# Two edits to a fused attention and mixture-of-experts kernel: a longer planned distance in the merge of routing and products, and a split last copy

## The chip, the cores and the metric

One NeuronCore of a Trainium2 chip runs the whole program. The time is the device time of one execution in microseconds (us). Five engines work side by side, each through its own instructions in program order: TensorE (PE in the profile), VectorE (DVE), ScalarE (ACT), GpSimd (POOL) and SyncE (SP, which here only starts loads). An instruction that waits holds back everything behind it on its engine.

## The reference, cut to what matters

```python
scores = np.where(mask, q @ k.T / 8, -1e9)     # 8 batches, 8 heads, 576 positions, window 64
x = (softmax(scores) @ v).reshape(4608, 512)
logits = x @ w_gate                            # 8 experts
for idx in np.argsort(-logits.flatten()):      # best (token, expert) pair first
    tok, e = idx // 8, idx % 8
    if assigned[tok] < 0 and counts[e] < 576:  # every expert takes 576 tokens
        assigned[tok] = e; counts[e] += 1
for e in range(8):
    out[assigned == e] = np.maximum(x[assigned == e] @ w1[e], 0) @ w2[e]   # 512 -> 1024 -> 512
```

## The kernel before

The first 165 us or so are the attention, which the change does not touch. After it, eight experts are closed one after the other. For the expert that fills up next, a **search** finds the threshold of its 576th token: four rounds, in each of which DVE compares all maxima with 15 thresholds (`G`, line 593), PE counts them in nine small matmuls (the tally, line 629), and DVE turns the counts into the next thresholds (lines 635 to 770). A **listing** then makes the 576 token numbers: PE sums positions (lines 931, 932), DVE and ACT build one-hot tables, PE multiplies them (18 matmuls, line 1020; 8 of line 1032), and DVE writes the list `idx` (line 1038). With the list, POOL gathers the tokens (`xg`, line 1202, five transfers). PE transposes them (`tp`, line 1240, four matmuls a tile) into one of two PSUM buffers (`bufs=2`), ACT copies the rounded high half out (`xh`, line 1190), and DVE subtracts it from the same `tp` to leave the low half (`xh`, line 1194). Tiles 0 and 1 are transposed as a pair, then 2 and 3, then 4.

An expert's **products** are the h layer (line 1302, in units: a 256-column unit has four 512-wide matmuls and four 256-wide ones) and the o layer: 16 matmuls of line 1336 and 96 of line 1346, all 512 wide. The first unit needs both halves of tiles 0 and 1. Weights come in 1024-column chunks: SP loads `st`, ACT copies the high half `wh` (line 1129) and starts the low half `wl` (line 1143), and an adding DMA that POOL starts completes `wl` (line 1145).

While PE works on the o layer of one expert, the listing of the next one ends and the search for the one after that begins; so rounds 1 to 4 of a search lie at the end of an o layer and in the h layer behind it.

The order of all this is made by a planner that runs when the program is built. `Streams` is a heap of generators; each yields the time that it believes its step takes, and whichever is due first issues its next instructions. `busy(dt, engine)` keeps one account for each engine and returns when the work would end. Due times are only an ordering device: on the chip each engine follows the order and waits where data are late. The planned costs that matter below, in ns: a 512-wide product 228, a pair of transposes 355 each, a tally 350, the matmuls of line 1020 630, those of line 1032 255, a copy of a weight chunk on ACT 1050, a copy of `xh` 520 on ACT and 600 on DVE; on the DMA account a gather or a put 700, a load 1350, an adding DMA 2650, with 2000 more until data land. POOL is charged 1300 for a gather, 1040 for a put, 650 for an adding DMA.

`SLACK[p]` is what the planner adds between a DVE step and the PE step that reads it, and between a PE step and the DVE step that reads it: twice in each tally (lines 624 and 633), in the listing of p at lines 929, 934, 1016, 1025, 1028 and 1036, and for p = 6 once more (line 969). The search that runs during expert p's products belongs to p + 1 and takes `SLACK[p + 1]`; the listing of p takes `SLACK[p]`. Of the places:

```python
yield max(slack, copied - self.clock() if not r else 0)   # tally, before the nine matmuls
yield self.busy(350) + 200 + slack                        # tally, before DVE reads the counts
yield self.dve(340) + slack                               # listing, before lines 931 and 932
yield self.busy(255) + 200 + slack                        # listing, before DVE writes idx
```

A tile pair is due by the gathers (`there`); then it waits until a routing matmul has been issued (`joins > n0`) or a latest time `t0` has come. The second copy of a pair is due 700 ns after the first:

```python
dt = self.busy(355)
self.spawn(evac(a, 128 if a < 4 else 64, t), dt + 150 + 700 * n)
```

Of the kernel before, what the change touches and what calls it, by code (L numbers as in the profile page):

```python
# [15 lines left out]
AF = mybir.ActivationFunctionType  # L16
# [7 lines left out]
E = 8  # L24
# [416 lines left out]
ALONE = [mybir.EngineType.DVE]  # L441
NG = 4
WIDE = 1.25
SLACK = (0, 0) + (100,) * 6
U32 = mybir.dt.uint32


class Routing:
# [297 lines left out]
    def guessed(self, p, code, one4, copied):  # L746

        nc, tile_ = self.nc, self.wk.tile
        tab, slack = self.gtab, SLACK[p]
        if p == 1:  # L750
# [124 lines left out]
    def steps(self, p):  # L875

        nc, wk, V = self.nc, self.wk, self.V
        m, best, one = self.m, self.best, self.one
        slack = SLACK[p]
        tile_ = wk.tile  # L880
# [179 lines left out]
JOIN = ((800, -1800), (2000, 900), (3300, 2000))  # L1060
SECOND = 27500
FIRST = 6500


class Experts:
# [29 lines left out]
    def load(self, p, ei):  # L1095
# [7 lines left out]
        def fetch(i):  # L1103
# [8 lines left out]
            if p == 0 and i == 3:  # L1112

                t = max(t, self.clock() + self.busy(0, "pool") + FIRST)
            there[i] = t
# [133 lines left out]
    def steps(self, p, idx):  # L1249
        nc, fw = self.nc, self.fw  # L1250
# [61 lines left out]
        def put(a, o):  # L1312
            ot = fw.tile([128, DM], FT, name="ot", bufs=3)
            m = 128 if a < 4 else 64
            if a < 4:
                nc.scalar.activation(ot, o, AF.Copy)  # L1316
                self.busy(500, "act")
            else:
                t = fw.tile([64, DM], FT, name="low")
                nc.scalar.activation(t, o[64:128], AF.Copy)  # L1320
                yield self.busy(500, "act") + 150
                self.busy(600, "dve")
                nc.vector.tensor_tensor(ot[0:64], o[0:64], t, OP.add)
            yield max(600, self.sent - self.clock())
            nc.gpsimd.indirect_dma_start(out=self.out[5 * p + a],  # L1325
                                         out_offset=IndirectOffsetOnAxis(ap=idx[0:m, a:a + 1], axis=0),
                                         in_=ot[0:m], in_offset=None)
            self.busy(TOKENS, "dma")
            self.sent = self.clock() + self.busy(1040, "pool")


        o = self.ps.tile([128, DM], FT, name="o", bufs=2)
        for f in range(NF):
            yield lambda: (p, NCH + f // 2) in self.W
            for n, w in enumerate(self.W[p, NCH + f // 2]):
                nc.tensor.matmul(o, hh[:, f, 512:], w[:, 512 * (f % 2):512 * (f % 2) + 512],  # L1336
                                 start=(f == 0 and n == 0), stop=(f == NF - 1 and n == 1))
                yield self.busy(228)
        self.spawn(put(4, o), 100)
        for a in range(4):  # L1340
            o = self.ps.tile([128, DM], FT, name="o", bufs=2)
            k = 0
            for f in range(NF):
                wh, wl = self.W[p, NCH + f // 2]
                for wt, ht in ((wh, hh), (wl, hh), (wh, hl)):
                    nc.tensor.matmul(o, ht[:, f, 128 * a:128 * a + 128], wt[:, 512 * (f % 2):512 * (f % 2) + 512],  # L1346
                                     start=(k == 0), stop=(k == 23))
                    k += 1
                    yield self.busy(228)
            self.spawn(put(a, o), 100)  # L1350
# [99 lines left out]
```

## Time and profile before

| | us |
|---|---|
| median of 3 runs | 622.74 (622.03 to 623.49) |
| the profiled execution | 619.33 |
| its span, first to last instruction | 617.4 |
| PE busy in the span | 591.4 (96%) |
| DVE, ACT, POOL busy | 397.6, 372.8, 186.2 |

The trace is of one execution, and all times of rows count from its first instruction. Matmuls overlap in it, so a busy PE is not a PE at its peak: a gap shows in the distance between the starts of successive matmuls.

### The profile page before, as it was taken

Reading aid. Unit: us, or ns where it says so; the run is one execution under the profiler, and the core shown is the slowest. Engines: PE = TensorE matmul, PEld = TensorE weight load, DVE = VectorE, ACT = ScalarE, POOL = GpSimd, SP = SyncE. Lnnn points to the kernel's source line nnn. Section 1 sums busy time; section 2 is a strip of 40 time slices with the busy share of each in tenths; the row PEclk is TensorE's granted clock in tenths of the full one; section 3 lists DMA queues with packets and bytes.
Section 4 is the critical chain, followed back from the end, with each engine's and each line's share of the span. In section 5 each row is a group of like instructions: output and inputs, shape, how many; then the busy total and the mean of one; then the engine's idle time right before and its main releaser. Section 6 shows DMA issues by size and latency. Waiting matters only on the chain.

```text
span 617.4 us, 15509 instructions
## 1 busy us (share of the span) xinstructions
PE 591.4 (96%) x5750; PEld 505.6 (82%) x5750; DVE 397.6 (64%) x1832; ACT 372.8 (60%) x798; POOL 186.2 (30%) x245
## 2 busy tenths in 40 slices
PE   8999899996599999999999999999999999999996
PEld 6777778785499789878987997898889789889984
DVE  6888888987786487468646846773695467705400
ACT  6998889996465387267537734762685275614410
POOL 1433445341341262044116203610630173011011
PEclk9999999998599999999999999999999999999998
DMA  8999999961598699189748937992896689410001
GB/s 315 358 363 365 362 390 376 355 223 71 158 254 179 216 209 251 34 299 224 171 143 239 247 75 255 210 235 68 270 240 124 200 214 316 184 44 34 2 27 51
DMA packets 44950, 128.85 MB, mean 209 GB/s; under 512 B 4672, under 2 KB 5312, under 8 KB 44864
## 3 DMA queue, kind: packets, MB, share of 16 engines
q1 hardware_dynamic: 30592, 79.00, 35.7%
q0 software_dynamic: 13984, 48.25, 33.8%
q8 instruction: 46, 0.75, 0.5%
q10 hardware_dynamic: 288, 0.52, 0.3%
q14 instruction: 40, 0.33, 0.2%
HBM read 82.14 MB, written 18.87 MB: 164 GB/s over the span
## 4 chain that ended last, share of the span: by engine, by line
PE 49%; issue 17%; DVE 4%; POOL 4%; DMA 1%; ACT 1%; POOLq 0%; DVEq 0%
PE h L1302 25%; PE o L1346 18%; PE o L1336 4%; POOL out L1325 2%; PE rps L629 1%; DVE xh L1194 1%; PE tp L1240 1%; POOL xg L1202 1%; POOL wl L1145 1%; DMA xg<-xs,idx 1%; PE rps L1020 1%; ACT xh L1190 0%; DMA xs<-x 0%; DVE G L593 0%; POOL rest L1202 0%
## 5 line engine op out<-in xcount | busy, mean ns | idle before, releaser
L1302 PE MATMUL h<-xh,wh 128*128 128x320 f32 (+2 forms) x800 | 160.9, 333 | 0.2 <-DVE xh L1194 0.2
L1302 PEld LDWEIGHTS h<-xh,wh 128*128 128x128 f32 x800 | 124.1, 188 | 5.1 <-DVE xh L1194 0.4
L1346 PE MATMUL o<-wh,hl 128*128 128x512 f32 x256 | 101.4, 396 | 0.0
L1346 PE MATMUL o<-wl,hh 128*128 128x512 f32 x256 | 100.5, 392 | 0.0
L1346 PE MATMUL o<-wh,hh 128*128 128x512 f32 x256 | 100.3, 392 | 0.0
L1325 POOL DMA_INDIRECT out<-ot,idx x40 | 40.1, 1003 | 198.5 <-DVE q L906 82.6
L141 ACT ACTIVATE pe<-st,mx 128x128 f32<-128x128 f32 x288 | 92.0, 393 | 5.2 <-DVE mx L136 4.9
L1302 PE MATMUL h<-xh,wl 128*128 128x256 f32 (+1 forms) x512 | 89.7, 296 | 0.0
L1302 PEld LDWEIGHTS h<-xh,wl 128*128 128x128 f32 x512 | 78.7, 188 | 4.4
L1145 POOL DMA_DIRECT2D wl<-st x51 | 46.0, 1024 | 83.6 <-ACT wl L1143 28.7
L1316 ACT ACTIVATE ot<-o 128x512 f32<-128x512 f32 x32 | 19.2, 598 | 83.2 <-PE o L1346 78.3
L1129 ACT ACTIVATE wh<-st 128x1024 fp32r<-128x1024 f32 x64 | 67.3, 1051 | 3.4 <-DMA st<-w 3.4
L136 DVE CUSTOM_DVE_ANT_0 st<-Sp,mask 128x128 f32<-128x128 f32 x288 | 63.8, 285 | 7.3 <-PE Sp L128 6.2
L1346 PEld LDWEIGHTS o<-wl,hh 128*128 128x128 f32 x256 | 48.1, 188 | 9.7
L1346 PEld LDWEIGHTS o<-wh,hh 128*128 128x128 f32 x256 | 48.1, 188 | 9.4
L1346 PEld LDWEIGHTS o<-wh,hl 128*128 128x128 f32 x256 | 48.1, 188 | 9.3
L1143 ACT ACTIVATE wl<-wh 128x1024 fp32r<-128x1024 f32 x51 | 54.0, 1058 | 1.1
L1266 ACT ACTIVATE hh<-h 128x320 fp32r<-128x320 f32 (+1 forms) x72 | 30.8, 428 | 30.9 <-PE h L1302 30.4
L1263 DVE TENSOR_TENSOR sum<-h,sum 128x256 f32<-128x256 f32 x56 | 23.6, 421 | 40.0 <-ACT sum L1261 38.6
L150 ACT ACTIVATE pt<-Tp 128x512 f32<-128x512 f32 x72 | 42.2, 587 | 8.3 <-PE Tp L148 8.3
L1202 POOL DMA_INDIRECT xg<-xs,idx x32 | 32.3, 1010 | 46.4 <-DVE eq L944 38.8
L1271 DVE SCALAR_TENSOR_TENSOR hl<-h,hh 128x256 fp32r<-128x256 f32 x72 | 30.3, 421 | 23.7 <-ACT hh L1266 23.5
(215 smaller groups left out, 1022.3 us busy)
## 6 DMA issues: line engine op xcount, KB each, us to landing
st<-w SPq DMA_DIRECT2D x59, 512.0 KB, 6.4
wl<-st POOLq DMA_DIRECT2D x51, 512.0 KB
xs<-x SPq DMA_DIRECT2D x36, 256.0 KB, 5.4
VO<-v SPq DMA_DIRECT2D x6, 1168.0 KB, 18.1
Q<-q SPq DMA_DIRECT2D x6, 1152.0 KB, 13.4
K<-k SPq DMA_DIRECT2D x6, 1152.0 KB, 16.3
VT<-vt SPq DMA_DIRECT2D x6, 1152.0 KB, 17.3
st<-w POOLq DMA_DIRECT2D x5, 512.0 KB
```

What stands on the lines that cost most here:

```text
L136: nc.vector.tensor_tensor_reduce(st[:, h, :], Sp[h % 2][:, h // 2], mk, scale=-0.125, scalar=3.0e38, op0=OP.add, op1=OP.min, accum_out=mx[ ...
L141: nc.scalar.activation(pe[:, h, :], st[:, h, :], AF.Exp, bias=mx[:, h:h + 1], scale=-1.0)
L150: return pt, lambda: nc.scalar.activation(pt.rearrange("p h q -> p (h q)"), Tp, AF.Copy)
L1129: nc.scalar.activation(hi, st[i], AF.Copy)
L1143: nc.scalar.activation(lo, hi.bitcast(FT), AF.Copy, scale=-1.0)
L1145: nc.gpsimd.dma_start(lo.bitcast(FT), st[i], accum_op=OP.add)
L1202: nc.gpsimd.indirect_dma_start(out=g[a][0:n], out_offset=None, in_=self.xs, in_offset=IndirectOffsetOnAxis(ap=idx[0:n, a:a + 1], axis=0))
L1266: nc.scalar.activation(hh[:, f, c0:c1], h, AF.Relu)
L1271: nc.vector.scalar_tensor_tensor(t, h[:, a - c0:b - c0], 0.0, hh[:, f, a:b].bitcast(FT), op0=OP.max, op1=OP.subtract)
L1302: nc.tensor.matmul(h[:, 0:w], wv[:, cc, 128 * (f % 2):128 * (f % 2) + 128], x[:, cc, x0:x0 + w], start=(k == 0), stop=(k == 4 * len(terms) ...
L1325: nc.gpsimd.indirect_dma_start(out=self.out[5 * p + a], out_offset=IndirectOffsetOnAxis(ap=idx[0:m, a:a + 1], axis=0), in_=ot[0:m], in_off ...
L1346: nc.tensor.matmul(o, ht[:, f, 128 * a:128 * a + 128], wt[:, 512 * (f % 2):512 * (f % 2) + 512], start=(k == 0), stop=(k == 23))
```

## The change

`SLACK` goes from 100 to 400 ns for p = 2 to 6 (third to seventh search and listing); p = 0, 1 and 7 keep their values. The last tile of the last expert (a = 3) is copied from PSUM in two halves of 256 columns, one by ACT and one by DVE, instead of whole by ACT.

```diff
-SLACK = (0, 0) + (100,) * 6
+SLACK = (0, 0) + (400,) * 5 + (100,)
...
+HALF = 256
...
             ot = fw.tile([128, DM], FT, name="ot", bufs=3)
             m = 128 if a < 4 else 64
-            if a < 4:
+            if p == E - 1 and a == 3:
+                nc.scalar.activation(ot[:, 0:HALF], o[:, 0:HALF], AF.Copy)
+                nc.vector.tensor_copy(ot[:, HALF:], o[:, HALF:])
+            elif a < 4:
                 nc.scalar.activation(ot, o, AF.Copy)
                 self.busy(500, "act")
```

## Rows read from the trace of the kernel before

**Rows 1.** The page: busy time, share of the span, instructions of PE.
```profile
PE 591.4 (96%) x5750; PEld 505.6 (82%) x5750; DVE 397.6 (64%) x1832; ACT 372.8 (60%) x798; POOL 186.2 (30%) x245
```

**Rows 2.** Timeline of PE, 264 to 300 us: start, length, instructions, idle before and releaser.
```profile
278.49 0.79 PE L1240 MATMUL tp<-identr,xg 128*128 128x128 f32 x8
...
282.27 0.79 PE L1240 MATMUL tp<-identr,xg 128*128 128x128 f32 x8
282.90 0.70 PE L1302 MATMUL h<-xh,wh 128*128 128x512 f32 x2
283.94 0.59 PE L629 MATMUL rps<-G,one 128*128 128x60 bf16 x9 [0.34 <-DVE G L593]
284.36 0.71 PE L1302 MATMUL h<-xh,wh 128*128 128x512 f32 x2
284.91 0.64 PE L1302 MATMUL h<-xh,wl 128*128 128x256 f32 x4
...
289.59 0.43 PE L629 MATMUL rps<-G,one 128*128 128x60 bf16 x9
289.85 0.39 PE L1302 MATMUL h<-xh,wh 128*128 128x320 f32 x1
```

**Rows 3.** Timeline of PE, 449 to 453 us: the same place three experts later.
```profile
451.24 0.59 PE L629 MATMUL rps<-G,one 128*128 128x60 bf16 x9 [0.31 <-DVE G L593]
```

**Rows 4.** The chain that ended last, 254 to 285 us: products between routing steps.
```profile
258.41 5.89 PE o L1346 x26
...
264.38 4.19 PE o L1346 x18
...
269.11 0.77 PE o L1346 x3
...
270.03 8.62 PE o L1346 x37
```

**Rows 5.** Timeline of ACT, 252 to 300 us: two copies of tokens, then weights.
```profile
279.16 1.09 ACT L1190 ACTIVATE xh<-tp 128x512 fp32r<-128x512 f32 x2 [1.37 <-PE tp L1240]
280.13 1.06 ACT L1129 ACTIVATE wh<-st 128x1024 fp32r<-128x1024 f32 x1
```

**Rows 6.** Timeline of DVE, 240 to 300 us: from first to second round.
```profile
279.79 0.69 DVE L1194 TENSOR_TENSOR xh<-tp,xh 128x512 fp32r<-128x512 f32 x1 [3.06 <-ACT xh L1190]
...
280.89 0.69 DVE L1194 TENSOR_TENSOR xh<-tp,xh 128x512 fp32r<-128x512 f32 x1
...
282.70 0.21 DVE L692 STREAM_TRANSPOSE num<-ps 128x32 f32<-128x32 f32 x1
282.94 0.16 DVE L768 TENSOR_REDUCE d<-num 128x1 f32<-128x8 f32 x1
...
283.41 0.79 DVE L593 TENSOR_TENSOR G<-m,thr 128x300 bf16<-128x300 f32 x2
```

**Rows 7.** Timeline of ACT, 533 to 538 us: weights between two copies of tokens.
```profile
533.95 1.05 ACT L1129 ACTIVATE wh<-st 128x1024 fp32r<-128x1024 f32 x1
534.90 0.59 ACT L1190 ACTIVATE xh<-tp 128x512 fp32r<-128x512 f32 x1
```

**Rows 8.** Timeline of PE, 536 to 538 us: a transpose that waits.
```profile
536.91 0.53 PE L1240 MATMUL tp<-identr,xg 128*128 128x128 f32 x4 [0.25 <-DVE xh L1194]
```

**Rows 9.** Timeline of POOL, 252 to 312 us: the first three adding DMAs.
```profile
277.85 2.85 POOL L1145 DMA_DIRECT2D wl<-st  x3
```

**Rows 10.** Timeline of PE, 501 to 508 us: the seventh expert.
```profile
501.41 0.79 PE L1240 MATMUL tp<-identr,xg 128*128 128x128 f32 x8
...
507.01 1.07 PE L1302 MATMUL h<-xh,wh 128*128 128x512 f32 x4
```

**Rows 11.** Timeline, 611 us to the end: the last copy.
```profile
611.34 0.60 ACT L1316 ACTIVATE ot<-o 128x512 f32<-128x512 f32 x1 [4.89 <-PE o L1346]
```

**Rows 12.** Groups by line: copies of half the width.
```profile
L1261 ACT ACTIVATE sum<-h 128x256 f32<-128x256 f32 x56 | 21.4, 382 | 29.5 <-PE h L1302 29.5
L1263 DVE TENSOR_TENSOR sum<-h,sum 128x256 f32<-128x256 f32 x56 | 23.6, 421 | 40.0 <-ACT sum L1261 38.6 <-issue 1.0
```

## The prediction

> **What bounds the kernel now.** I read the page first, then the waits of PE, then PE's timeline around each place where PE waits, then ACT and DVE at the same times. On the page the reader is to see that PE is busy for 96% of the span [rows 1]: only PE's gaps can give time back, and anything that makes PE wait costs in full. In the o and h layers the gap worth seeing is before the second round's tally. The h layer opens at 282.90 with two products; at 0.227 us each the tally could begin at 283.36 and be over 0.26 later, as the third round's is (289.59 to 289.85). It begins at 283.94, waits in its middle for the second half of `G`, and the next product starts at 284.36 instead of 283.62 [rows 2]. I take 0.7 us (0.65 to 0.74) for this stall. The same place three experts later shows the same releaser [rows 3]; there are four of them, in the o layers of the second to fifth expert. All four together are 2.8 us, and that is the most that a longer distance can recover. The third round shows no wait, and neither does any other tally from the third search on.
>
> **The change: what is moved.** I work out the order from the planner's rules, counting due times from S, the start of an o layer, in us. They say only what stands before what. Before: lines 931 and 932 are due at 9.41, line 1020 at 13.81, line 1032 at 15.07, the list at 15.70, the first pair of transposes and the first tally at 23.61. With a product each 0.228 that puts 16 + 26, 18, 3 and 37 products between them, which is what the chain has [rows 4]. So the rules can be trusted for the order after.
>
> After, each distance is 0.3 longer: 9.71, 14.64, 16.58, and the list at 17.60, 1.9 late (six distances and the rounding to whole products). Everything that hangs on the list is late too: gathers, transposes, and the next search.
>
> The first tally is due 17.60 + 7.28 (DVE's work up to it) + 0.40 = 25.28. The first pair of transposes now stands right behind it, after 107 products of the o layer instead of 100. Then come five products, the second pair (28.89), the first h products (held in the plan until 29.75 for the weights), and the second tally at 31.16, behind nine h products instead of two. On ACT, the copy of tile 0 is due at 26.29 and that of tile 1 at 27.34 (tally and transposes end at 26.49, plus 0.85). The high copy of the fourth weight chunk is due at 18.75 (list, plus one low copy of 1.15), plus what the DMA account then holds: five gathers from 17.60 end at 21.10, an adding DMA at 23.75, the load at 25.10, landed at 27.10. So this copy slips between the two token copies; before, with 24.34, 25.40 and 25.90, it came behind both, as ACT's timeline shows [rows 5]. On DVE the subtraction of tile 1 falls from just behind `sq` to 28.83, behind `num` (28.50) and ahead of `d` (28.93).
>
> **The change: what it costs.** Now chip times, in the cycle shown. The first pair starts 7 products and a tally later: 278.49 + 1.59 + 0.26 = 280.34. ACT's first copy starts 0.67 after the transposes (278.49 to 279.16) [rows 2, 5], at 281.01. The weight copy starts 0.48 later (half the distance from 279.16 to 280.13) [rows 5], at 281.49, tile 1's copy another 0.95 later [rows 7], at 282.44, done at 283.04. DVE starts tile 0's low half 0.63 after ACT's copy started (279.16 to 279.79), at 281.64, done at 282.33. From the start of such a subtraction (280.89) to the end of `num` (282.91) it is 2.02 [rows 6], so tile 1's subtraction starts at 283.6 and ends at 284.3.
>
> What waits for it is new. The `tp` buffers are two: tile 3 takes the buffer that tile 1 leaves when this subtraction is done. The trace has one such wait, behind the same ACT order of token copy, weight copy, token copy: the second tile of a pair starts when DVE's `xh` ends [rows 8]. PE is free for tile 3 at 282.27 + 0.32 = 282.59 (the work up to there is the same) and starts it at 284.35, so the h layer begins 1.76 us late, at 284.66 instead of 282.90. The first unit needs the same subtraction, so it would wait there in any case.
>
> The old stall goes: nine h products (four at 0.227, four at 0.12, one at 0.227) bring PE to the second tally at 286.3, and `G` is done 1.26 after `d` starts (282.94 to 284.20) [rows 6], at about 285.5. Net for one cycle: +1.76 - 0.7 = +1.05. The four cycles give +4.2.
>
> The sixth o layer, where the seventh expert is prepared, has no search. There the first pair moves nine products back, 501.41 to 503.45; by the same steps tile 1's low half is done at 507.0, and the h layer starts at about 507.55 instead of 507.01 [rows 10]: +0.55. In the first o layer only the tallies move, into h products; no stall there, nothing gained.
>
> Costed at nothing: the adding DMA of the first weight chunk, at 277.85, 7.06 before its first use at 284.91 [rows 2, 9]. Gathers begin 1.6 late (seven products stand ahead of line 1032 more than before), but one put moves from behind to ahead of them, so the DMA is 0.65 late while its use is 1.76 late; without that put's move it would be 0.9 later and still covered. The later listing of the last expert is idle time for POOL either way.
>
> The last copy: whole it takes 0.60 [rows 11]; ACT's half is 0.38, and DVE's nearest row, a 256-wide operation on PSUM with two operands, 0.42 [rows 12]. POOL waits for both: -0.2. Bounds: -0.22, and +0.2 if the halves run one after the other (0.38 + 0.42). I take -0.2, since no row shows either engine held up by the other.
> The Trainium skill ("PSUM — Partial Sum Buffer", section "PSUM bank collisions raise a hardware error") speaks against this edit: ScalarE and VectorE must not read one bank on the same partitions at once, and the compiler orders such accesses. By that rule the halves follow each other and the edit costs 0.2 instead of giving it; no row of this trace has the two engines reading one tile at once.
>
> Sum: +4.2 + 0.55 - 0.2 = +4.5. On the profiled execution that is 619.33 + 4.5 = 623.9; the runs shown lie 3.4 above it (622.74), so the median forecast is **627.2**, with a range of its own from 626 to 629. A measurement of this kernel can tell about 0.2%, 1.25 us, from no change.
>
> **The rivals.**
> *Faster.* The four stalls go and nothing takes their place: -2.8 - 0.2 = -3.0, some 619.7. Everything turns on one place, the subtraction of tile 1: if it ends before 282.6, PE never sees it. For it: the second and third rounds' margin does grow. Against it: the first pair can't come before 280.3, and from transposes to subtraction the rows of before already take 3.1 (278.49 to 281.58), which gives 283.4.
> *Nearly cancelled.* The weight copy stays behind both token copies. Its margin in the plan is 0.24 (27.10 against 27.34). Then tile 1's subtraction ends at about 283.3, the h layer is 0.8 late, the stall of 0.7 goes but 0.3 of wait for `G` is left, since DVE has the same work to do: some +0.4 a cycle and +0.2 in the sixth, +1.6 in all, 624.3; with the wait for `G` gone too it is within 1.25.
> *Worse.* The margin of the subtraction ahead of `d` is 0.10. If it falls behind `thr`, it is 0.45 later, and with it the h layer: +1.8 over the four cycles, 629.0 in all.
> *No effect.* The tallies might keep their places, so that the releaser in [rows 2] stays: 622.5. Against it: 0.3 is more than one product, so they must move.
>
> **How the numbers follow.** Chances: the forecast 0.60, worse 0.11, nearly cancelled 0.10 (half of it within 0.2%), no effect 0.04, faster 0.15. Hence slower by over 0.2% 0.60 + 0.11 + 0.05 = 0.76, within 0.2% 0.09, faster 0.15. Most of the chance is of one sign. The range reaches down through the nearly cancelled case and no effect, and up to the worse one: 621.8 to 629.6. It leaves out the faster case and some of the worse.
>
> **What would show it.** Right: in the second to fifth o layers, a transpose of line 1240 that waits for DVE `xh` with more than 1 us, four times; no wait of line 629 for `G`; ACT with `wh` between two copies of `xh`; the first pair after the first tally; the list some 1.6 later. Wrong: the h layer starting where it did, with the tally's wait gone (faster); both the transposes' and the tally's wait (worse). The forecast fails if the order on ACT or DVE differs by one place from what I worked out, or if DVE gets through its ten small steps in less than the 2.02 shown.

## The result, and the profile after

The changed kernel takes 628.0 us (median of 6 runs, 627.17 to 630.84) against 623.38 us before (6 runs, 622.03 to 624.45): a ratio of 1.0084, 95% interval 1.0059 to 1.0109. That is 5.2 us slower (3.7 to 6.8). The ratio and its interval come from all the runs and not from the two medians, which lie 4.6 us apart. The forecast was 4.5 us slower. The profiled execution took 627.81 us, its span 626.1.

The chain that ended last, in the second expert's o layer (start, length, engine and line, number of instructions): what was 26, 18, 3 and 37 products [rows 4] is now

```profile
260.91 6.12 PE o L1350 x27
...
267.11 4.87 PE o L1350 x21
...
272.52 1.47 PE o L1350 x6
...
274.14 8.65 PE o L1350 x37
```

Lines from 1063 on are moved by one, those from 1316 on by four. The list is written seven products later, and the first token pair comes after 27 + 21 + 6 + 37 = 91 products of line 1350 and the 16 of line 1340: 107, where it was 100. The timeline of PE there (start, length, instructions, idle time before and its releaser):

```profile
282.67 0.42 PE L629 MATMUL rps<-G,one 128*128 128x60 bf16 x9
282.93 0.86 PE L1241 MATMUL tp<-identr,xg 128*128 128x128 f32 x8
...
284.85 0.54 PE L1241 MATMUL tp<-identr,xg 128*128 128x128 f32 x4
286.77 0.54 PE L1241 MATMUL tp<-identr,xg 128*128 128x128 f32 x4 [1.38 <-DVE xh L1195]
287.14 1.16 PE L1303 MATMUL h<-xh,wh 128*128 128x512 f32 x4
...
288.84 0.43 PE L629 MATMUL rps<-G,one 128*128 128x60 bf16 x9
289.11 0.72 PE L1303 MATMUL h<-xh,wh 128*128 128x512 f32 x2
```

The reader is to see two things against [rows 2]. The four transposes of tile 3 are torn from those of tile 2 and wait 1.38 us for DVE's `xh`. And the second tally no longer waits: it stands behind nine h products and costs 0.27 us. PE's waits count the first of these in a group (in total, times, longest):

```profile
PE tp L1241 <- DVE xh L1195: 5.8, 5, 1.4
```

Four of the five are this place in the four cycles; the fifth, 0.3 us, is the place of [rows 8], which waited before as well. No line of that view names line 629 any more. The timeline of ACT at the same time, the answer to [rows 5]:

```profile
283.48 0.60 ACT L1191 ACTIVATE xh<-tp 128x512 fp32r<-128x512 f32 x1 [2.18 <-PE tp L1241]
283.97 1.06 ACT L1130 ACTIVATE wh<-st 128x1024 fp32r<-128x1024 f32 x1
284.92 0.59 ACT L1191 ACTIVATE xh<-tp 128x512 fp32r<-128x512 f32 x1
```

and of DVE, the answer to [rows 6]:

```profile
284.11 0.69 DVE L1195 TENSOR_TENSOR xh<-tp,xh 128x512 fp32r<-128x512 f32 x1 [0.39 <-issue]
...
285.93 0.21 DVE L692 STREAM_TRANSPOSE num<-ps 128x32 f32<-128x32 f32 x1
286.06 0.65 DVE L1195 TENSOR_TENSOR xh<-tp,xh 128x512 fp32r<-128x512 f32 x1
286.63 0.15 DVE L768 TENSOR_REDUCE d<-num 128x1 f32<-128x8 f32 x1
...
287.08 0.79 DVE L593 TENSOR_TENSOR G<-m,thr 128x300 bf16<-128x300 f32 x2
```

The weight copy lies between the two token copies, and the subtraction of tile 1 behind `num`. It ends at 286.71, and tile 3 starts at 286.77. ACT was done with tile 1 at 285.51, so the last 0.55 us ahead of the subtraction are DVE's small steps.

The last copy, the answer to [rows 11]; the timeline of ACT, DVE and POOL:

```profile
619.45 0.38 ACT L1317 ACTIVATE ot<-o 128x256 f32<-128x256 f32 x1 [4.89 <-PE o L1350]
619.87 0.42 DVE L1318 COPY ot<-o 128x256 f32<-128x256 f32 x1 [20.91 <-ACT ot L1317]
620.57 0.96 POOL L1329 DMA_INDIRECT out<-ot,idx  x1 [4.77 <-DVE ot L1318]
```

DVE had been idle for 20.91 us and still started only when ACT's half was over. From ACT's start to the scatter it is 1.12 us; before, it was 0.87.

By layers, worked out from PE's timeline as the distance between the first products of successive layers (us; the experiments of the next section stand beside the two kernels):

| kernel | o layer, 2nd to 5th expert | h layer behind it | o layer of the 6th |
|---|---|---|---|
| before | 28.31 to 28.36 | 27.41 to 27.44 | 29.37 |
| changed | 30.05 to 30.09 | 26.77 to 26.79 | 30.61 |
| slack_only | 30.04 to 30.06 | 26.78 to 26.79 | 30.69 |
| listing_only | 30.03 to 30.06 | 26.77 to 26.80 | 30.71 |
| tally_only | 28.31 to 28.36 | 27.27 to 27.39 | 29.44 |
| copy_only | 28.31 to 28.36 | 27.55 to 27.63 | 29.48 |
| pair_closer | 29.07 to 29.12 | 26.89 to 26.91 | 29.84 |
| rounds_later | 28.31 to 28.36 | 26.78 | 29.37 |

On average each of the four cycles is 1.73 us longer in its o layer and 0.65 shorter in its h layer: +1.1, or +4.3 in all. The sixth o layer adds 1.24, the last copy 0.25, and the stretch behind the last scatter 0.3 (5.50 us instead of 5.21). The two profiled spans lie 8.7 us apart, more than the medians, because the stretch ahead of the second o layer took 2.5 us longer in the later execution. The change is not the cause of that: tally_only and copy_only, which keep this stretch's order on PE but for three tallies (one to three h products later) or for nothing, show 257.92 and 257.22 for the start of that layer, the changed kernel 257.10, the kernel before 254.59.

### The profile page after: what moved, and what is told of

Read it like the earlier page. It is cut to its first block, busy times and chain, and to the rows that moved or that the text cites. A ratio compares the mean times of both kernels' runs of the same rounds, so it can differ in the third digit from the quotient of the medians.

```text
span 626.1 us, 15519 instructions
## 1 busy us (share of the span) xinstructions
PE 592.4 (95%) x5750; PEld 505.5 (81%) x5750; DVE 397.3 (63%) x1833; ACT 370.7 (59%) x798; POOL 185.9 (30%) x245
## 4 chain that ended last, share of the span: by engine, by line
PE 47%; issue 19%; POOL 4%; DMA 2%; DVE 2%; ACT 1%; POOLq 0%
PE h L1303 24%; PE o L1350 17%; PE o L1340 4%; POOL out L1329 2%; POOL xg L1203 1%; PE tp L1241 1%; DMA rest<-xs,idx 1%; PE rps L629 1%; DVE xh L1195 1%; POOL wl L1146 1%; DMA out<-ot,idx 1%; PE rps L1020 0%; DMA xs<-x 0%; ACT xh L1191 0%; POOL rest L1203 0%
## 5 line engine op out<-in xcount | busy, mean ns | idle before, releaser
L1350 PE MATMUL o<-wh,hl 128*128 128x512 f32 x256 | 100.0, 391 | 0.0
L176 PE MATMUL Op<-VO,pt 128*64 128x73 f32 x608 | 43.1, 230 | 0.7 <-DVE best L566 0.3
L128 PE MATMUL Sp<-K,Q 64*64 64x128 f32 x1152 | 41.6, 280 | 0.9 <-issue 0.5
```

The source lines that it names most:

```text
L128: nc.tensor.matmul(Sp[r][64 * a:64 * a + 64, pp], Q[b][d, i, p], K[b][d, k0:k0 + 2, p], start=True, stop=True)
L176: nc.tensor.matmul(Op[g][64 * a:64 * a + 64, h, :], pt[:, h, 64 * a:64 * a + 64], vv[a][:, 4 * g + h, :], start=True, stop=True)
```

## Experiments

All are compared with the kernel before on the same chip; the first four share its runs (median 623.41), and so do the last four (median 620.77).

**The longer distance alone.**

```diff
-SLACK = (0, 0) + (100,) * 6
+SLACK = (0, 0) + (400,) * 5 + (100,)
```

> The longer distance alone, the last copy as before. Theory A (late list, subtraction of tile 1 behind num on DVE, third token tile waits for its buffer): a wait of about 1.4 us at line 1240 in four o layers, no wait of line 629 for G, and the time of the whole change less its copy edit: +4.5 to +5.5 us, ratio 1.007 to 1.009. Rival B (much of the loss is the serial halves of the last copy, or a difference between executions): under +2.5 us, ratio below 1.004.

Measured: 628.73 us, ratio 1.0094 (1.0067 to 1.0121). The wait at line 1240 is 1.38 us at the place shown above, and the layers are those of the changed kernel. The distance alone makes the loss: 5.9 us by the ratio, a little above what was expected.

**The split copy alone.**

```diff
+            if p == E - 1 and a == 3:
+                nc.scalar.activation(ot[:, 0:HALF], o[:, 0:HALF], AF.Copy)
+                nc.vector.tensor_copy(ot[:, HALF:], o[:, HALF:])
```

> The split last copy alone, all distances as before. The forecast's term: -0.2 us. The profile of the changed kernel, where DVE's half starts only when ACT's half is over: +0.2 to +0.3 us, ratio about 1.0004, with 1.1 us from the start of ACT's copy to the start of the last scatter against 0.87 before. Either way within what can be measured; the profile decides between the two.

Measured: 623.92 us, ratio 1.0009 (0.999 to 1.0028). The time can't decide, the profile does: again 1.12 us from ACT's start to the scatter against 0.87. The edit costs 0.25 us.

**The tallies alone.**

```diff
-        tab, slack = self.gtab, SLACK[p]
+        tab, slack = self.gtab, 400 if 2 <= p <= 6 else SLACK[p]
```

> 400 ns in the tallies of the third to seventh search alone, the listings at 100, last copy as before. Theory A: the list and the token copies keep their places, so no wait at line 1240; the second tally stands behind three h products instead of two, so the wait for G shrinks by 0.23 us in each of four layers: -0.9 us, ratio 0.9985. Rival B (the longer tallies themselves make the loss, by a later search): slower by 2 us or more.

Measured: 623.02 us, ratio 0.9996 (0.9975 to 1.0017). The timeline of PE:

```profile
286.23 0.93 PE L1302 MATMUL h<-xh,wh 128*128 128x512 f32 x3
287.45 0.59 PE L629 MATMUL rps<-G,one 128*128 128x60 bf16 x9 [0.29 <-DVE G L593]
```

Three products instead of two, and PE still waits for `G`: behind the third product the tally could start at 286.91. The h layers are some 0.25 us shorter than copy_only's, which kept the old order on the same chip; 1 us in all, as theory A has it, and too little for the time to show. The o layers are untouched, so rival B falls: the tallies make no loss.

**The listings alone.** With the first diff above:

```diff
-        tab, slack = self.gtab, SLACK[p]
+        tab, slack = self.gtab, 100 if 2 <= p <= 6 else SLACK[p]
```

> 400 ns in the listings of the third to seventh expert alone, the tallies at 100, last copy as before. Theory A: the list is late as in the whole change; tile 1 is subtracted behind thr on DVE, line 1240 waits about 1.3 to 1.4 us, and the second tally, behind three h products, finds G ready because the h layer starts late: +4.5 us, ratio 1.007, all of the loss without the tallies. Rival B (the tallies make the loss): within 0.2% of before.

Measured: 628.24 us, ratio 1.0078 (1.0052 to 1.0104). The timeline of PE, and below it that of DVE:

```profile
286.90 0.54 PE L1240 MATMUL tp<-identr,xg 128*128 128x128 f32 x4 [1.36 <-DVE xh L1194]
287.29 0.93 PE L1302 MATMUL h<-xh,wh 128*128 128x512 f32 x3
288.05 0.43 PE L629 MATMUL rps<-G,one 128*128 128x60 bf16 x9
```

```profile
286.01 0.23 DVE L770 SCALAR_TENSOR_TENSOR thr<-gtab,d,base 128x15 f32<-128x15 f32 x1
286.16 0.68 DVE L1194 TENSOR_TENSOR xh<-tp,xh 128x512 fp32r<-128x512 f32 x1
286.76 0.78 DVE L593 TENSOR_TENSOR G<-m,thr 128x300 bf16<-128x300 f32 x2
```

The listing's distance makes the loss without any of the tallies'. The old wait for `G` goes here too, with the tally behind only three products: the h layer now opens so late that `G` is ready. What the changed kernel gets back in its h layers is thus no fruit of the longer tally distance either.

**The token pair closer together.** With the first diff above:

```diff
-                self.spawn(evac(a, 128 if a < 4 else 64, t), dt + 150 + 700 * n)
+                self.spawn(evac(a, 128 if a < 4 else 64, t), dt + 150 + (300 if p > 1 else 700) * n)
```

> The longer distance everywhere, but the second copy of a token pair due 300 ns after the first instead of 700, so that ACT copies both tiles before the weight chunk and DVE subtracts tile 1 behind cnt instead of behind num. Theory A (PE waits for that subtraction and nothing else): the wait at line 1240 falls from 1.4 to about 0.5 us, a wait for G of up to 0.3 us stays, and of the loss of about 5 us some 2 are left: ratio 1.002 to 1.005. Rival B (tile 3 waits for its gather or the weights, not for DVE): no change from the kernel with the longer distance, ratio 1.008 to 1.009.

Measured: 623.18 us, ratio 1.0043 (1.0023 to 1.0063): 2.7 us of loss. The timeline of PE:

```profile
285.83 0.53 PE L1240 MATMUL tp<-identr,xg 128*128 128x128 f32 x4
286.82 0.53 PE L1240 MATMUL tp<-identr,xg 128*128 128x128 f32 x4 [0.46 <-DVE xh L1194]
287.19 1.16 PE L1302 MATMUL h<-xh,wh 128*128 128x512 f32 x4
288.19 0.63 PE L1302 MATMUL h<-xh,wl 128*128 128x256 f32 x4
288.67 0.55 PE L629 MATMUL rps<-G,one 128*128 128x60 bf16 x9
```

The list comes as late as with the distance alone, 17.1 us into the o layer. Only the places of tile 1's two steps have moved, its copy ahead of the weight copy on ACT and its subtraction behind `cnt` on DVE (it starts at 286.07), and the wait falls from 1.38 to 0.46. Rival B falls with it: the gathers hang on the same late list, and the weight copy starts 0.48 us later in the layer than with the distance alone. The o layer is 0.95 us shorter than there; that kernel ran on the other chip, but the o layers of the old order are equal on both. Some 0.1 us of the wait for `G` stays in the h layer.

One part of the gain is no repair of the change. The closer pair holds for the eighth expert's tokens too, and the o layer in which they are prepared, the seventh, takes 27.26 us here against 27.68 to 27.73 in every other kernel of this document: the wait of [rows 8] is gone. The closer pair with the old distances was not tried.

**Only rounds 2 to 4 later.** All distances as before, but:

```diff
-        yield max(slack, copied - self.clock() if not r else 0)
+        yield max(slack, copied - self.clock()) if not r or one4 is None or slack < 100 else 1000
```

> Distances of 100 as before, but the tallies of rounds 2 to 4 of the third to seventh search are due 1000 ns after DVE's compare; listings, token copies and last copy as before. Theory A: the second tally stands behind more h products, PE no longer waits for G, nothing else moves: 4 x 0.65 to 0.8, or -2.6 to -3.2 us, ratio 0.995 to 0.996. Rival B (something else is late at the same place, so the wait only changes its name): the time of before within 0.2%.

Measured: 619.1 us, ratio 0.9976 (0.9959 to 0.9993): faster than the kernel before, by 1.5 us (0.4 to 2.5). The timeline of PE:

```profile
284.71 0.79 PE L1240 MATMUL tp<-identr,xg 128*128 128x128 f32 x8
285.34 1.16 PE L1302 MATMUL h<-xh,wh 128*128 128x512 f32 x4
286.34 0.52 PE L1302 MATMUL h<-xh,wl 128*128 128x256 f32 x3
286.70 0.43 PE L629 MATMUL rps<-G,one 128*128 128x60 bf16 x9
```

The o layers stay at 28.31 to 28.36 and the h layers fall to 26.78, with neither wait. Theory A named the mechanism; its size was too large, since on this chip the old order has h layers of 27.25 to 27.31 (the next two kernels keep it), so the stall that goes is 0.5 us, not 0.65 to 0.8. Four times 0.5 is 2.0.

**Which thing keeps the two engines apart.** Two kernels at the last tile, distances as before, one execution each. In the first, ACT copies the whole tile, and DVE copies half of it once more into an unused buffer:

```diff
                 nc.scalar.activation(ot, o, AF.Copy)
+                if p == E - 1 and a == 3:
+                    junk = fw.tile([128, 256], FT, name="sum", bufs=4)
+                    nc.vector.tensor_copy(junk, o[:, 256:])
```

> As before, and at the last tile DVE also copies half of the same PSUM tile into a buffer that nobody reads, while ACT copies the whole tile as before. Theory A (the two engines are kept apart because they read one PSUM tile): DVE's copy starts when ACT's is over, some 0.6 us after ACT's start. Rival B (they are kept apart because both halves write one SBUF tile): DVE's copy starts with ACT's, within 0.1 us. Time as before within 0.2% either way.

The timeline of ACT and DVE:

```profile
612.73 0.60 ACT L1316 ACTIVATE ot<-o 128x512 f32<-128x512 f32 x1 [4.89 <-PE o L1349]
613.36 0.42 DVE L1320 COPY sum<-o 128x256 f32<-128x256 f32 x1 [21.13 <-ACT ot L1316]
```

It took 620.44 us; the kernel before took 618.81 to 624.65 on this chip. DVE waits for ACT though it writes another buffer: it is the PSUM tile that they share. In the second, the halves of the changed kernel are partitions instead of columns:

```diff
-                nc.scalar.activation(ot[:, 0:HALF], o[:, 0:HALF], AF.Copy)
-                nc.vector.tensor_copy(ot[:, HALF:], o[:, HALF:])
+                nc.scalar.activation(ot[0:64], o[0:64], AF.Copy)
+                nc.vector.tensor_copy(ot[64:128], o[64:128])
```

> Distances as before; the last tile is copied in halves of 64 partitions with all 512 columns, the lower by ACT and the upper by DVE. Theory A (kept apart by PSUM bank and partitions): the halves run side by side, 0.7 us from ACT's start to DVE's end. Rival B (kept apart by whole tile): one after the other, 0.60 + 0.68 = 1.3 us. Time within 0.2% of before either way.

The timeline of ACT and DVE:

```profile
613.62 0.59 ACT L1317 ACTIVATE ot<-o 64x512 f32<-64x512 f32 x1 [4.89 <-PE o L1350]
614.24 0.69 DVE L1318 COPY ot<-o 64x512 f32<-64x512 f32 x1 [21.12 <-ACT ot L1317]
```

It took 622.59 us, again one execution within that range. One after the other again, 1.31 us: disjoint partitions do not let them run side by side. Whether they are kept apart by the tile or by the PSUM bank in which it lies is not shown, since no run gave the two engines two tiles of one bank.

## Why the prediction held

**The order.** Right in all that it counted: 107 products ahead of the first pair and five behind it, the first pair behind the first tally, the weight copy between the token copies, the subtraction between `num` and `d`, nine h products ahead of the second tally.

**The new wait.** Forecast +1.76 us a cycle, measured +1.73. The step on which it rested held: from the start of tile 0's subtraction (284.11) to the end of `num` (286.14) it is 2.03, against 2.02 in the sum (six small steps lie behind the subtraction there, not the ten that the forecast names). pair_closer shows that the wait hangs on the place of this subtraction. That the first h products would wait for it even with a third `tp` buffer was argued, not tried.

**The old stall.** Forecast -0.7, measured -0.65 on the traces compared. The stall itself lies at the head of the h layers, not in the o layers where the forecast counts the four of them. The experiments add that it is not of one size (0.5 to 0.8, see the end), and that either of two things alone ends it: a late h layer with only three products ahead of the tally (listing_only), or more products ahead of it with the h layer on time (rounds_later).

**The sixth o layer.** The mechanism was right, and the size off: +0.55 in the sum, +1.24 measured. The timeline of PE:

```profile
510.33 0.80 PE L1241 MATMUL tp<-identr,xg 128*128 128x128 f32 x8
512.68 0.69 PE L1020 MATMUL rps<-B,R 128*128 128x64 bf16 x18 [0.32 <-DVE R L1012]
513.20 0.51 PE L1241 MATMUL tp<-identr,xg 128*128 128x128 f32 x4
514.49 0.51 PE L1241 MATMUL tp<-identr,xg 128*128 128x128 f32 x4 [0.77 <-PE tp L1241]
```

and of ACT and DVE:

```profile
510.87 0.89 ACT L1004 ACTIVATE R<-A,lane 128x648 bf16<-128x648 bf16 x1 [3.42 <-DVE A L1002]
511.65 0.58 ACT L1191 ACTIVATE xh<-tp 128x512 fp32r<-128x512 f32 x1
513.07 0.59 ACT L1191 ACTIVATE xh<-tp 128x512 fp32r<-128x512 f32 x1
513.70 0.69 DVE L1195 TENSOR_TENSOR xh<-tp,xh 128x512 fp32r<-128x512 f32 x1
```

Tile 3 starts at 514.49, 0.1 us after the subtraction of tile 1 ends (514.39), so that wait is the one that was worked out, though the profile names a transpose as its releaser. The term that was mis-sized is in "by the same steps": ACT's first copy starts 1.32 us after the transposes began, where the steps of the cycle have 0.67; that is 0.65 of the 0.69 us by which the term fell short. The copy stands on ACT behind that engine's part of the table `R`, which waits for DVE's `A` and through it for `Y`, and `Y` started 0.81 us after its matmul, against 0.24 in the trace of before. In pair_closer, where `Y` starts after 0.24, the same copy starts 0.77 after the transposes; that `Y` accounts for most of the excess is argued from this, not tried. In the old order a late `Y` costs little: copy_only has one of 0.84 and a sixth o layer of 29.48, against 29.37. The wait of line 1020 for `R` adds nothing of its own, as PE waits for tile 3 behind it in any case.

**The last copy.** The step that failed: "I take -0.2, since no row shows either engine held up by the other." It is +0.25, a little beyond the upper bound of +0.2. The sentence of the Trainium skill ("PSUM — Partial Sum Buffer", section "PSUM bank collisions raise a hardware error") had the sign right, and the trace agrees: DVE starts 0.42 us after ACT, when ACT's half is over. Where that page lets engines into different quadrants of one bank at once, the build of this kernel doesn't use it: rows_split stays serial, with 0.62 us between the starts. That no row showed an operation was no reason to take the better bound.

**The sum.** With the sizes of the two main traces it is 4.3 + 1.24 + 0.25 + 0.3 = 6.1, inside the interval of 3.7 to 6.8. Two traces that are known to be of one chip, slack_only against copy_only, give 3.7 for the four cycles and 1.21 for the sixth o layer; with the last copy and the 0.3 us at the end that is 5.5. The forecast's 4.5 was near because most of it lay in the four cycles, where the term was right; what it missed (the sixth o layer, the last copy and the 0.3 us at the end, which it did not have) all lay on the slow side. Of the rivals, *faster* is what rounds_later does without the listing's distance, and *nearly cancelled* is what pair_closer made, at 2.7 us where 1.6 had been worked out.

## What to carry to other kernels

In this kernel a longer planned distance paid only at the step whose wait the profile shows, one tally a cycle: 1000 ns at it and the two tallies behind it gave 1.5 us, while 300 ns more at every step of a chain of fourteen took 5, and the six steps of the listing alone took as much. A chain that is off the critical path still sets when everything hung on it falls due; work out what the late part will stand behind on the other engines' queues, and whose buffer that holds. When a copy is to be shared by two engines, look first at whether they may read the tile together.

## What was not expected of the hardware

Two engines that read disjoint halves of one PSUM tile ran one after the other, by columns (0.42 us between the starts) and by partitions (0.62 us). The profile names ACT's copy as what released DVE's, so the order is one that the program as built keeps; what the engines would do without it no run shows. And the same instructions can take different times, the same ones each time: for the last listing `Y` starts 0.80 to 0.90 us after line 932's matmul in the first four experiments, which shared a chip, and in the changed kernel, and 0.24 us after it in the last four, which shared another, and in the kernel before. The old stall, as an h layer less 26.78, is 0.8 us in copy_only and 0.5 to 0.65 in the second group. Two chips would explain both; which chip the two main traces come from is not recorded. Also, from the last scatter's start to the end it is 5.2 us in every kernel whose listings keep their distance and 5.5 in the four whose listings have the longer one; the cause of these 0.3 us stays open.
